# One fused attention and feed-forward kernel, its planner's cost of tiling changes on TensorE and of weight-load issues, and an order made anew

## The chip, the cores and the metric

The kernel runs on one core of one Trainium2 chip. The metric is the device time of one execution in microseconds (us). The kernel before took 1262.62 us, the median of three runs (1257.67 to 1267.32).

## The reference

Masked attention over 8 batches, 8 heads, 576 positions and 64 features, and behind it a feed-forward layer with a rational activation (512 to 2048 to 512):

```python
scores = scale * np.matmul(q, k.transpose(0, 1, 3, 2))
thresh = np.max(scores, axis=-1, keepdims=True) - tau
scores = np.where(scores >= thresh, scores, -1000000000.0)
...
attn = attn / (np.sum(attn, axis=-1, keepdims=True) + 1e-09)
return np.matmul(attn, v).astype(np.float32)
...
h = x @ w_in
P = a[0] + a[1] * h + a[2] * h2 + a[3] * h3
Q = 1.0 + np.abs(b[0]) * np.abs(h) + np.abs(b[1]) * h2
g = P / (Q + 1e-06)
return (g @ w_out).astype(np.float32)
```

Here x is the attention output with the heads laid side by side, 4608 rows of 512. All inputs and the output are float32.

## The kernel before, in words

**Work.** Heads are taken in pairs; `bp` counts the 32 pairs (8 batches of 4). The 576 positions are four tiles of 128 and a remainder of 64. One *unit* is one pair and one tile of 128 query positions (`unit_ops`). Its score matmuls (`f_qk`, line 810) contract over 64 features, so each of the two heads uses 64 rows of TensorE: the profile shows the form 64*128. The remainder units (line 800) hold both heads in one weight tile and run as 128*128. VectorE takes the row maxima (L818), ScalarE subtracts and masks (L833) and takes the exponential with its sum (L837). The scaled probabilities are split into a high and a low half-precision part: `hi` on ScalarE (L347) or VectorE (L349), the low part on VectorE (L859). Both are transposed by DMAs on SyncE's queue (`f_tp`, L869). For the first pairs (`is_plain`) the transposition runs on TensorE instead (`f_tr`, L882 and L887) and is copied out of PSUM (`f_ev`). The weighted sum over V (`f_av`, L928; `f_avp`, L912) fills 64 columns for each head: the form 128*64. It is made for two full tiles together.

The feed-forward layer takes 256 rows at a time (`moe_ops`): the first matmul (`f_g1`, L1045) uses w_in as high and low halves, a chain of VectorE and ScalarE operations (L1054 to L1095) makes the rational function, and the second matmul (`f_g2`, L1104) uses w_out in two float32 parts. The weights arrive as 64-bit words: `decode_ops` loads a tile of them by a DMA on GpSimd's queue (`load`, L546 and L582) and turns it into float32 on ScalarE and VectorE, in buffers of the pool `t` that the feed-forward chain uses later. `scale_ops` finds power-of-two scales by a maximum, a diagonal matrix (L442) and one small matmul (`f_all`, L446).

**Order.** No operation is emitted when it is written down. `op(engine, duration, key, function, ...)` records it, with the operations it needs, the buffers it takes and those it gives back. `Plan.order` then simulates the engines: at each step it takes, for each engine, the operation that can start first (with ties inside `TOL` decided by the smaller key), and emits them in that order. The order on each engine and on each DMA queue is therefore fixed in advance, and the chip executes each queue in order. An operation's key is its position in the series of units plus a number from the table `TURN` (one for each call of `begin`: one for each weight tile, V load, Q and K load, unit and feed-forward step) and one from `KIND` (one for each sort of operation), both in thousandths of a unit.

**Choice of engine.** An operation listed in `FLEX` can go to ScalarE or VectorE. `sooner` compares, for both, the start plus the duration times that engine's price: `EARLY` before the planned time `EARLY_END`, `PRICE` behind it.

**Durations.** Before the change a score unit is booked with 1.36 us (remainder: 1.12), a weighted sum with 1.86 us (remainder 0.69; in the plain form 2.36 and 0.76), whatever stands beside it. A weight load is booked with 2.5 us on the issuing queue `GD`, 1.9 us (times 1.25) on the wire and 2.0 us (plus 0.3) to its landing. `f_warm` (L1248) fills planned idle time of TensorE with small matmuls up to the planned time 400.

Of the kernel before, what the change touches and what calls it, by code (L numbers as in the profile page):

```python
# [77 lines left out]
        "ev": {"ACT": 0.465, "DVE": 0.6}, "ev1": {"ACT": 0.156, "DVE": 0.196}, "A": {"ACT": 0.565, "DVE": 0.341},  # L78
        "gh": {"ACT": 0.51, "DVE": 0.33}, "wh": {"ACT": 0.57, "DVE": 0.38}}

EARLY = {"ACT": 1.6309, "DVE": 3.9296}
EARLY_END = 714.5248
PRICE = {"ACT": 0.9171, "DVE": 2.3360}

TURN = [
# [22 lines left out]
KIND = [  # L108
# [4 lines left out]

TOL = {"PE": 0, "ACT": 0.129, "DVE": 0.1, "POOL": 0.1, "DMA": 0, "GD": 0}
WARM, WARM_ONE, WARM_LONG, WARM_END = 0.6, 0.22, 3.0, 400.0

BEGIN = 1.4
WIRE, LATER = 1.25, 0.3


# [20 lines left out]
class Plan:  # L141
# [17 lines left out]
    def pool(self, name, n):  # L159
        self.pools[name] = [(0.0, i) for i in range(n)]  # L160

    def op(self, eng, dur, key, fn, after=(), take=(), drop=(), wire=None):
        engs = {eng: dur} if isinstance(eng, str) else eng
        o = Op(engs, key, fn, [x for x in after if x is not None], list(take), list(drop))
        o.wire = wire and (wire[0] * WIRE, wire[1] + LATER)
        o.turn, o.kind = self.turn, self.kinds.setdefault(fn.__code__, len(self.kinds))
        turn = TURN[o.turn] / 1000 if o.turn < len(TURN) else 0.0
        o.key += turn
        o.key += KIND[o.kind] / 1000 if o.kind < len(KIND) else 0.0
        o.rank = self.rank + turn  # L170
        self.ops.append(o)
        return o
# [20 lines left out]
    def order(self):  # L193
# [16 lines left out]
                if h.pool in line:  # L210
                    line[h.pool].append(h)
        done, busy = [], dict.fromkeys(engines, 0.0)
        left, wire = len(self.ops), 0.0
        while left:
            best = None
            for e in engines:
# [11 lines left out]
                if not starts:  # L228
                    continue
                first = min(t for t, _ in starts)  # L230
                starts = sorted([x for x in starts if x[0] <= first + TOL[e]] if all(len(o.engs) == 1 for _, o in starts)
                                else starts, key=lambda x: (x[1].key, x[1].n))
# [4 lines left out]
                first = min(t for t, _ in keep)  # L237
                t, o = min(((t, o) for t, o in keep if t <= first + TOL[e]), key=lambda x: (x[1].key, x[1].n))
# [2 lines left out]
            assert best is not None, "no op can start"  # L241
            t, o, e = best
            o.eng, o.dur = e, o.engs[e]
            for x in o.engs:
                can[x].remove(o)
            if e == "PE" and self.warm is not None and t < WARM_END:
# [10 lines left out]
            if o.wire is not None:  # L257
                wire = max(wire, t + BEGIN) + o.wire[0]
# [39 lines left out]
def masked_attention_rational_ffn(  # L298
# [27 lines left out]
    op = plan.op  # L326
# [156 lines left out]
    def decode_ops(i, key, load, hold, dst=None):  # L483


        box = {}
        plan.begin(key - AHEAD_RANK)
        ht = Hold("u", 1)

        def ld():  # L490
            if not loaded:

                for x in KKs[0][:, 0:1], QQs[0][:, 0:1]:
                    nc.gpsimd.tensor_scalar(cf[:, 15:16], x, 1.0, 1.0, ALU.mult, ALU.mult)
            if len(loaded) >= AHEAD and plan.now - loaded[-AHEAD][1] < RECENT:


                nc.gpsimd.tensor_scalar(cf[0:1, 15:16], loaded[-AHEAD][0][0:1, 0, 1:2].bitcast(F32), 1.0, 1.0, ALU.mult, ALU.mult)
            box["rw"] = load()
            loaded.append((box["rw"], plan.now))  # L500

        def f1():


            box["w"] = place(ht)
            nc.scalar.activation(box["w"], box["rw"][:, :, 1].bitcast(F32), AF.Prelu, scale=REBIAS, alpha=-2.0 ** 32)

        def f2():
            nc.scalar.activation(box["rw"][:, :, 0], box["rw"][:, :, 0].bitcast(U32), AF.Copy, scale=2.0 ** -29)

        def f4():
            t = box["w"].bitcast(I32)
            nc.vector.tensor_single_scalar(t, t, 3, ALU.logical_shift_left)

        def f6():
            t = box["w"].bitcast(I32)
            if dst is None:
                tensor_tensor(box["rw"][:, :, 1], t, box["rw"][:, :, 0], ALU.add)
                box["w"] = box["rw"][:, :, 1].bitcast(F32)
            else:  # L520
                tensor_tensor(dst.bitcast(I32), t, box["rw"][:, :, 0], ALU.add)

        l = op("GD", 2.5, key - 2.0, ld, (), [hold], wire=(1.9, 2.0))
        if i < NC:
            first_loads.append(l)
        o1 = op("ACT", 0.567, key, f1, [l], [ht])
        o2 = op("ACT", 0.568, key, f2, [l])
        o4 = op("DVE", 0.335, key, f4, [o1])
        o6 = op(FLEX["f6"], 0, key, f6, [o4, o2], (), [ht] if dst is None else [ht, hold])
        return o6, box  # L530
# [7 lines left out]
    for i in range(NW):  # L538
        pieces = []
        for c in range(NC):  # L540
            n = i * NC + c
            hold = Hold("t", 1)
# [5 lines left out]
            key = w_key(i, c)  # L548
# [8 lines left out]
        key = w_key(i, NC)  # L557
# [19 lines left out]
    for f in range(NF):  # L577
        hold = Hold("t", 1)
# [5 lines left out]
        key = w_key(f // NC, NC + f % NC)  # L584
# [88 lines left out]
    def v_low(bp):  # L673
        if bp not in v_done:
            p, o, vl, vc, vhi = v_ops[bp]
            o = op(FLEX["vl"], 0, p + 0.1, vl, [o] + plain_av.get(bp, []))
            v_done[bp] = op("DVE", 0.25, p + 0.15, vc, [o], (), [vhi])
        return v_done[bp]
# [88 lines left out]
    def unit_ops(bp, t):  # L767
# [180 lines left out]
        sh = dict.fromkeys(heads, Hold("s", nh, B2 if single else B3))  # L948
        ex, mk = {}, {}
        need = k_done[bp] + q_done[bp]  # L950
        qk = op("PE", 1.36 if full else 1.12, p, f_qk, need, [sh[0]], [kh, qh] * nh)
        if full:
            mx = op("DVE", 1.255, p + 0.1, lambda: f_max(None), [qk], [st_hold])
        else:
# [40 lines left out]
            xh_hold[ck] = Hold("x" if ck[0] == "m" else "xr", 8 * NFP)  # L995
            first = [xh_hold[ck]]
        if plain:
            av = op("PE", 2.36 if full else 0.76, p + 1.2, f_avp, two["tp"] + [v_loaded[bp], x_first.get(ck)], [bh] + first, [two["pT"], vh_[bp]])
            plain_av.setdefault(bp, []).append(av)
        else:  # L1000
            av = op("PE", 1.86 if full else 0.69, p + 1.2, f_av, two["tp"] + [v_low(bp), x_first.get(ck)], [bh] + first, [two["pT"], vh_[bp]])
        x_first.setdefault(ck, av)
        xh = op(FLEX["xh" if full else "xhr"], 0, p + 1.4, f_xh, [av, isx_done["up"]] + ([x_done[ck][0]] if not first else []), (), [bh])
        xl = op("DVE", 0.335 if full else 0.134, p + 1.5, f_xl, [xh], (), [bh])
# [286 lines left out]
```

## Time and profile before

| | |
|---|---|
| median of three runs | 1262.62 us (1257.67 to 1267.32) |
| the profiled execution | 1266.8 us, span 1265.0 us |
| mean granted TensorE clock in it | 0.991 |
| matmul instructions on TensorE | 9650, as many weight loads |
| packets moved by DMA | 338603, 138.54 MB |

The span goes from the first to the last instruction of the profiled execution; its own time holds a little more, and it is one execution, not the median. Lines are those of the kernel file; the helpers `times` (L347 on ScalarE, L349 on VectorE) and `copy` (L339, L341) record one line for all who call them. A float32 matmul stands in the trace as two records, one in half precision as one. Matmuls overlap, so the time that a run of them takes is read from its start to the start of what follows.

### The profile page before, as it was taken

Reading aid. Unit: us, or ns where it says so; the run is one execution under the profiler, and the core shown is the slowest. Engines: PE = TensorE matmul, PEld = TensorE weight load, DVE = VectorE, ACT = ScalarE, POOL = GpSimd, SP = SyncE. Lnnn points to the kernel's source line nnn. Section 1 sums busy time; section 2 is a strip of 40 time slices with the busy share of each in tenths; the row PEclk is TensorE's granted clock in tenths of the full one; section 3 lists DMA queues with packets and bytes.
Section 4 is the critical chain, followed back from the end, with each engine's and each line's share of the span. In section 5 each row is a group of like instructions: output and inputs, shape, how many; then the busy total and the mean of one; then the engine's idle time right before and its main releaser. Section 6 shows DMA issues by size and latency. Waiting matters only on the chain. (4 is left out here: it accounts for less than half of the span.)

```text
span 1265.0 us, 25738 instructions
## 1 busy us (share of the span) xinstructions
PE 1226.9 (97%) x9650; PEld 961.6 (76%) x9650; DVE 1188.0 (94%) x1830; ACT 1118.3 (88%) x2185; POOL 97.8 (8%) x217
## 2 busy tenths in 40 slices
PE   8899999999999999999999999999999989999998
PEld 6677777777777777767777777777777767778886
DVE  6999899999999999999999899999999979998787
ACT  7999999999989899988898999899999979895564
POOL 4110000010001100101001100021001100000000
PEclk9999999999999999999999999999999989999999
DMA  6454644675556654665664666667456664542000
GB/s 193 136 167 129 149 81 85 134 151 119 114 95 146 126 110 102 124 121 89 124 116 80 131 125 96 122 120 139 90 112 125 132 109 88 116 88 45 18 17 17
DMA packets 338603, 138.54 MB, mean 110 GB/s; under 512 B 312624, under 2 KB 321712, under 8 KB 338480
## 3 DMA queue, kind: packets, MB, share of 16 engines
q1 hardware_dynamic: 326656, 103.40, 43.9%
q0 software_dynamic: 11072, 32.91, 8.9%
q8 instruction: 76, 1.25, 0.4%
q10 hardware_dynamic: 752, 0.59, 0.2%
q14 instruction: 47, 0.39, 0.1%
HBM read 52.17 MB, written 9.44 MB: 49 GB/s over the span
## 5 line engine op out<-in xcount | busy, mean ns | idle before, releaser
L1104 PE MATMUL banks<-wp,g 128*128 128x512 f32 x1728 | 449.1, 408 | 3.2 <-DVE g L1095 1.7
L1104 PEld LDWEIGHTS banks<-wp,g 128*128 128x128 f32 x1728 | 317.1, 191 | 82.6 <-DVE g L1095 4.4
L1045 PEld LDWEIGHTS <-wi 128*128 128x128 f16 x3456 | 328.8, 98 | 65.3 <-issue 23.3
L1045 PE MATMUL banks<-x,wi 128*128 128x256 f16 x3072 | 360.4, 274 | 3.8 <-ACT t L1054 3.3
L837 ACT ACTIVATE e<-e,cf 128x576 f32<-128x576 f32 x288 | 222.3, 779 | 0.2
L859 DVE SCALAR_TENSOR_TENSOR e<-e,st,hi 128x576 f16<-128x576 f32 x252 | 204.3, 811 | 7.2 <-ACT hi L347 6.5
L833 ACT ACTIVATE e<-banks,st 128x576 f32<-128x576 f32 x288 | 207.2, 739 | 4.2 <-DMA pT<-e 1.9
L347 ACT ACTIVATE hi<-e,st 128x576 f16<-128x576 f32 x225 | 171.0, 770 | 30.2 <-DVE st L848 25.3
L810 PE MATMUL banks<-KK,QQ 64*128 64x64 f32 (+1 forms) x1024 | 175.5, 455 | 7.4 <-ACT e L833 4.5
L818 DVE TENSOR_REDUCE st<-banks 128x2 f32<-128x1152 f32 x128 | 172.3, 1346 | 8.0 <-PE banks L810 7.2
L810 PEld LDWEIGHTS banks<-KK,QQ 64*128 64x128 f32 x1024 | 115.1, 188 | 77.0 <-issue 46.9
L1054 ACT ACTIVATE t<-banks,hsc 128x512 f32<-128x512 f32 (+1 forms) x192 | 106.6, 577 | 26.0 <-PE banks L1045 16.4
L928 PE MATMUL banks<-pT,V 128*64 128x256 f16 (+1 forms) x2520 | 121.7, 250 | 2.6 <-DVE xr L944 2.4
L928 PEld LDWEIGHTS <-V 128*64 128x64 f16 x2520 | 103.7, 111 | 23.3 <-issue 18.8
L1081 DVE SCALAR_TENSOR_TENSOR t<-t,co,t 128x1024 f32<-128x1024 f32 (+1 forms) x73 | 92.2, 1263 | 18.7 <-ACT t L1075 18.6
L1072 ACT ACTIVATE t<-t,co 128x1024 f32<-128x1024 f32 (+1 forms) x73 | 82.9, 1136 | 28.3 <-DVE t L1078 27.0
L1095 DVE TENSOR_TENSOR g<-t,g 128x512 fp32r<-128x512 f32 x144 | 95.2, 683 | 0.8 <-ACT g L339 0.7
L1087 DVE SCALAR_TENSOR_TENSOR t<-t,co,t 128x1024 f32<-128x1024 f32 (+1 forms) x73 | 92.2, 1264 | 0.6
L1065 DVE SCALAR_TENSOR_TENSOR t<-t,co 128x1024 f32<-128x1024 f32 (+1 forms) x73 | 92.2, 1263 | 0.3 <-ACT t L1054 0.3
L1068 DVE SCALAR_TENSOR_TENSOR t<-t,co 128x1024 f32<-128x1024 f32 (+1 forms) x73 | 92.2, 1263 | 0.0
L1078 DVE SCALAR_TENSOR_TENSOR t<-t,co,t 128x1024 f32<-128x1024 f32 (+1 forms) x73 | 92.2, 1263 | 0.0
L1084 DVE SCALAR_TENSOR_TENSOR t<-t,t 128x1024 f32<-128x1024 f32 (+1 forms) x73 | 87.9, 1204 | 0.5
(116 smaller groups left out, 1183.5 us busy)
## 6 DMA issues: line engine op xcount, KB each, us to landing
KK<-in_kT_dram SPq DMA_DIRECT2D x108, 144.0 KB, 3.0
t<-in_w_in_dram POOLq DMA_DIRECT2D x16, 512.0 KB, 4.9
t<-in_w_out_dram POOLq DMA_DIRECT2D x16, 512.0 KB, 4.8
V<-in_v_dram POOLq DMA_DIRECT2D x28, 256.0 KB, 4.4
out_dram<-u POOLq DMA_DIRECT2D x26, 256.0 KB, 3.0
QQ<-in_qT_dram SPq DMA_DIRECT2D x72, 64.0 KB, 2.3
pT<-hi SPq DMA_TRANSPOSE x140, 3.3
pT<-e SPq DMA_TRANSPOSE x140, 3.3
```

What stands on the lines that cost most here:

```text
L347: nc.scalar.activation(dst, src, AF.Identity, scale=factor)
L810: mm = nc.tensor.matmul(s[:, d0:d0 + n], QQ[r, t * P:(t + 1) * P], KK[r, k0:k0 + n], **one)
L818: nc.vector.tensor_reduce(box["st"][:, 0:2], box["both"], AX.X, ALU.max, negate=True)
L833: nc.scalar.activation(ev(hh), box["s"][hh], AF.Prelu, scale=SCALE, bias=box["st"][:, 2 + hh:3 + hh], alpha=STEEP)
L837: nc.scalar.activation(e, e, AF.Exp, scale=passes, accum_out=box["st"][:, 4 + hh:5 + hh])
L859: nc.vector.scalar_tensor_tensor(box["lo"][:, c], ev(hh), box["st"][:, 6 + hh:7 + hh], box["hi"][:, c], ALU.mult, ALU.subtract)
L928: nc.tensor.matmul(dst, V[:, c * P + hh * D:c * P + (hh + 1) * D], rhs, start=c == 0 and n == 0, stop=c == NT and n == 2)
L1045: nc.tensor.matmul(d, wi_tile(c, f0 + j, hl), x[:, c, :], start=c == 0 and n == 0, stop=c == NC - 1 and n == 2)
L1054: nc.scalar.activation(box["h3"][:, 2 * k:2 * k + 2, sl], psv[:, :, sl], AF.Identity, scale=hsc[:, b2, g:g + 1])
L1065: nc.vector.scalar_tensor_tensor(box["r"], box["h"], a2, box["h"], ALU.add, ALU.mult)
L1095: nc.vector.tensor_tensor(fr(g[:, 1]), box["r"][:, k * GW:(k + 1) * GW], g[:, 0], ALU.subtract)
L1104: nc.tensor.matmul(acc[tt], fr(g[:, x]), fr(wo[f][y]), start=begins and j == n == 0, stop=ends and j == nb - 1 and n == 2)
```

## The change

The planner gets a cost for a change of TensorE's tiling. Each operation has a `mode`: 1 for score units, 2 for weighted sums, 0 for all others. When TensorE's next operation has another mode than the last, `TURNS` = 0.093 us is added to its duration. The booked durations of score units and weighted sums are each lowered by 0.185 us (about twice 0.093). A weight load is booked with 0.65 us on the issuing queue instead of 2.5, and with 0.3 us more to the landing. The tables `TURN` (367 numbers) and `KIND` (65) and the four prices are replaced, so that the order on all engines is a new one. No emitted operation is edited.

```diff
-EARLY = {"ACT": 1.6309, "DVE": 3.9296}
+EARLY = {"ACT": 1.7163, "DVE": 3.8382}
 EARLY_END = 714.5248
-PRICE = {"ACT": 0.9171, "DVE": 2.3360}
+PRICE = {"ACT": 1.0826, "DVE": 2.3926}
...
+TURNS = 0.093
...
-    def op(self, eng, dur, key, fn, after=(), take=(), drop=(), wire=None):
+    def op(self, eng, dur, key, fn, after=(), take=(), drop=(), wire=None, mode=0):
...
+        o.mode = mode
...
-        left, wire = len(self.ops), 0.0
+        left, wire, mode = len(self.ops), 0.0, 0
...
             o.eng, o.dur = e, o.engs[e]
+            if e == "PE":
+                o.dur += TURNS if o.mode != mode else 0.0
+                mode = o.mode
...
-        l = op("GD", 2.5, key - 2.0, ld, (), [hold], wire=(1.9, 2.0))
+        l = op("GD", 0.65, key - 2.0, ld, (), [hold], wire=(1.9, 2.3))
...
-        qk = op("PE", 1.36 if full else 1.12, p, f_qk, need, [sh[0]], [kh, qh] * nh)
+        qk = op("PE", 1.175 if full else 0.935, p, f_qk, need, [sh[0]], [kh, qh] * nh, mode=1)
...
-            av = op("PE", 2.36 if full else 0.76, p + 1.2, f_avp, two["tp"] + [v_loaded[bp], x_first.get(ck)], [bh] + first, [two["pT"], vh_[bp]])
+            av = op("PE", 2.175 if full else 0.575, p + 1.2, f_avp, two["tp"] + [v_loaded[bp], x_first.get(ck)], [bh] + first, [two["pT"], vh_[bp]], mode=2)
...
-            av = op("PE", 1.86 if full else 0.69, p + 1.2, f_av, two["tp"] + [v_low(bp), x_first.get(ck)], [bh] + first, [two["pT"], vh_[bp]])
+            av = op("PE", 1.675 if full else 0.505, p + 1.2, f_av, two["tp"] + [v_low(bp), x_first.get(ck)], [bh] + first, [two["pT"], vh_[bp]], mode=2)
```

Of the tables, the entries of the same kinds before and after show how far keys move (thousandths of a unit): score units -1392 and -1418, weighted sums -1204 and -4381, the first feed-forward matmul 152 and -1087, the second 727 and 215.

52 rows, old and new, of tables (KIND, TURN) are left out of this document.

## The prediction

> **What bounds the kernel now.** I read the page's busy times first, then busy time by stage, then the clock inside short stretches, TensorE's waits, and its instructions in order of time.
>
> ```profile
> span 1265.0 us, 25738 instructions
> PE 1226.9 (97%) x9650; PEld 961.6 (76%) x9650; DVE 1188.0 (94%) x1830; ACT 1118.3 (88%) x2185; POOL 97.8 (8%) x217
> ```
>
> The stage table (start:end, length, then busy time of TensorE, its weight loads, VectorE, ScalarE and GpSimd, with the number of instructions in brackets, the granted TensorE clock, the DMA share and GB/s) shows where the missing 3% lies:
>
> ```profile
> 0.00:217.00 217.00, 200.81 (x1531) 157.34 (x1531) 195.18 (x416) 203.34 (x432) 29.06 (x65) 0.99 0.52 137
> 217.00:1014.00 797.00, 784.64 (x6377) 612.52 (x6377) 776.32 (x1134) 737.89 (x1441) 66.53 (x148) 0.99 0.61 117
> 1014.00:1030.00 16.00, 11.74 (x61) 8.62 (x61) 11.29 (x24) 9.11 (x19) 0.00 (x0) 0.79 0.90 147
> 1030.00:1260.00 230.00, 229.23 (x1684) 183.10 (x1682) 205.17 (x259) 167.28 (x297) 2.21 (x4) 1.00 0.28 55
> ```
>
> TensorE is busy for 229.23 of the 230 us from 1030 to 1260, where its work ends, so every microsecond taken off its queue there or earlier comes off the end. It idles 217.00 - 200.81 = 16.2 us in the first stage, 797.00 - 784.64 = 12.4 us in the second and 4.3 us in the third. VectorE follows closely: in the second stage it is only 784.64 - 776.32 = 8.3 us less busy than TensorE. So TensorE is the bound, with VectorE right behind it.
>
> The waits behind those gaps (engine, line, whom it waited for, us in total, times, longest):
>
> ```profile
> PE banks L446 <- DVE u L442: 4.9, 2, 4.3
> PE banks L810 <- ACT e L833: 4.5, 9, 1.7
> PE banks L882 <- ACT pT L339: 3.4, 5, 1.1
> PE banks L1045 <- ACT t L1054: 3.3, 3, 1.8
> PE banks L810 <- DMA KK<-in_kT_dram: 2.6, 2, 2.1
> PE banks L928 <- DVE xr L944: 2.4, 1, 2.4
> ```
>
> They are a few long ones, each of another kind, not a steady drip. Each is followed by a stretch of low clock (eighth column here: the granted clock, after the five busy times):
>
> ```profile
> 559.00:564.00 5.00, 5.00 (x39) 3.35 (x35) 4.95 (x9) 2.72 (x5) 0.00 (x0) 0.66 0.35 69
> 692.00:697.00 5.00, 5.00 (x35) 3.97 (x28) 4.46 (x7) 3.57 (x10) 2.12 (x5) 0.66 0.94 181
> 744.00:748.00 4.00, 3.48 (x9) 2.84 (x10) 4.00 (x8) 3.55 (x7) 2.16 (x4) 0.57 0.86 203
> 1020.00:1028.00 8.00, 6.67 (x27) 4.89 (x28) 7.12 (x19) 6.78 (x14) 0.00 (x0) 0.57 0.75 164
> ```
>
> Lost clock is length x (1 - clock): 1.7 + 1.7 + 1.7 + 3.4 = 8.5 us. With the idle 12.4 + 4.3 = 16.7 us, the middle of the kernel (217 to 1030) loses 25.2 us to stalls, in four clusters of about 6 us.
>
> **The change, part by part.** No instruction is added or taken away by the edit itself, except that the number of filler matmuls (L1248) follows the planner's gaps. What changes is the order on every engine, and which of two engines takes an optional operation.
>
> First, the tiling changes. TensorE in order of time (start, us, line, count of records; the first and last tiled runs enclose a gapless stretch):
>
> ```profile
> 4.66 5.30 PE L810 MATMUL banks<-KK,QQ 64*128 64x64 f32 x16
> ...
> 311.82 1.35 PE L810 MATMUL banks<-KK,QQ 64*128 64x64 f32 x8
> 313.10 1.48 PE L1045 MATMUL banks<-x,wi 128*128 128x256 f16 x12
> 314.34 3.05 PE L1104 MATMUL banks<-wp,g 128*128 128x512 f32 x12
> 317.31 1.83 PE L928 MATMUL banks<-pT,V 128*64 128x256 f16 x30
> 319.07 1.35 PE L810 MATMUL banks<-KK,QQ 64*128 64x64 f32 x8
> 320.35 3.07 PE L1104 MATMUL banks<-wp,g 128*128 128x512 f32 x12
> 323.26 3.45 PE L1045 MATMUL banks<-x,wi 128*128 128x256 f16 x30
> 326.64 1.83 PE L928 MATMUL banks<-pT,V 128*64 128x256 f16 x30
> 328.40 1.35 PE L810 MATMUL banks<-KK,QQ 64*128 64x64 f32 x8
> 329.68 4.10 PE L1045 MATMUL banks<-x,wi 128*128 128x256 f16 x36
> 333.54 1.17 PE L1104 MATMUL banks<-wp,g 128*128 128x512 f32 x3
> ...
> 1154.79 1.83 PE L928 MATMUL banks<-pT,V 128*64 128x256 f16 x30
> 1156.55 3.06 PE L1104 MATMUL banks<-wp,g 128*128 128x512 f32 x12
> ```
>
> I take the time of a run as its start to the next run's start. A score unit (L810) takes 1.27 to 1.28 us and a weighted sum (L928, full) 1.76 us, whether a tiled or an untiled run stands ahead or behind. So leaving a tiling costs nothing beyond what those two figures hold. Entering does: L1045 takes 3.86 us for 36 and 1.24 us for 12 ahead of L1104, 0.109 us each, so 30 would take 3.20; ahead of the weighted sum 30 take 3.38, 0.17 us more. L1104 x12 takes 2.91 us ahead of L1045 and 2.97 ahead of the weighted sum, 0.06 more. A tiled run placed directly behind another therefore saves 0.06 to 0.17 us. Where the untiled neighbours stand about evenly I take 0.13 for one saved entry, from the upper part of that span, because the second L1104 figure follows an L1045 run and the first does not.
>
> [...]
>
> How many entries? Over the whole timeline, from the row at 4.66 to that at 1154.79, I count 224 runs of score units and weighted sums, 176 of them entered from an untiled run and 48 directly behind another tiled one. If every run had one tiled neighbour, 112 entries would be left: 64 x 0.13 = 8.3 us is the most, and none is the least. The pick among ready operations on TensorE does not look at the tiling; the new cost is added after the pick. Pairs arise only because the keys are new. So I take about half, 35 entries, and 35 x 0.13 = 4.5 us off.
>
> The accounting is not quite the chip's. The remainder scores are counted as tiled like the others, though the trace has them as 128*128:
>
> ```profile
> L800 PE MATMUL banks<-KK,QQ 128*128 128x512 f32 x64 | 33.4, 604 | 0.3 <-ACT st L842 0.3
> L1248 PE MATMUL banks<-ident 128*128 128x128 f32 x162 | 26.4, 309 | 1.4 <-POOL ident masks.py:199 1.4
> ```
>
> With two records of this form a unit these are 32 units: if each is placed as a free neighbour and is not one, at most 32 x 0.13 = 4.2 us of the credit is false. I take this as contained in "half".
>
> Second, the weight loads. The planner now books 0.65 us instead of 2.5 us on the issuing queue for each of 32 loads, and 0.3 us more to the landing. The trace has
>
> ```profile
> 63.73 0.53 POOL L582 DMA_DIRECT2D t<-in_w_out_dram  x1 [13.67 <-ACT t L509]
> ...
> POOL t L546 <- ACT t L509: 18.1, 1, 18.1
> ```
>
> An issue takes 0.53 us, so the new figure is the better one; but the queue waits for buffers that ScalarE and VectorE have to give back, up to 18.1 us at once, and no row of TensorE's waits names a weight load. Earlier issue is covered by that wait. I cost it at nothing. If the cover went and an earlier weight load delayed a load of V, K or Q, the nearest row is the 2.1 us that scores waited for K: bounds -2 and +2 us. In the same first stage the filler matmuls take 26.4 us and the idle time is 16.2 us; a new order can shift some of this either way, and I take nothing, bounds -5 and +5.
>
> Third, the order itself. V loads, Q and K loads, scale computations and whole units move on every queue, so the four clusters of stalls will not come at the same places. For the long one (4.3 us at L446) the scale matmul stood in TensorE's queue ahead of operations that were ready, with the whole queue behind it waiting for VectorE's L442; for the next K load it was SP's queue in which the transposes stood ahead. A moved operation meets the same in-order queues, so new waits arise too. Bounds: none left, -25.2 us; as many again, +25.2 us. I take half a cluster, -3 us, nearer to no change, because nothing in the cost model that touches those four waits is altered.
>
> Fourth, the prices. Where an operation may go to either engine, its time is weighed by EARLY (first part) or PRICE. VectorE's price over ScalarE's goes from 2.41 to 2.24 and from 2.55 to 2.21: a little more work for VectorE, below its slack of 8.3 us. I take nothing; the far end is the third rival.
>
> Sum: 1266.8 us for the profiled execution (span 1265.0 and 1.8 around it) - 4.5 - 3 = 1259.3. That execution lies 4.2 us above the median of the runs, 1262.62, so against the median the forecast is 1255.1 us.
>
> **The rivals.** (1) It does not do what it says: the pick ignores the tiling, TensorE's runs are paired as before, and stalls return in other places at the same total: 1262.6 us. For it speaks that a unit's scores become ready only when ScalarE (L833) has freed its banks, so that pairs are set by readiness; against it, that 48 pairs stand already.
>
> (2) The stalls go: three of the four middle clusters don't return, 0.75 x 25.2 = 18.9 us, with the 4.5 us of entries: 1262.6 - 23.4 = 1239.2 us. For it: the stretch from 1030 to 1260 runs nearly without a gap. Against it: each cluster has its own cause. [...]
>
> (3) Slower: VectorE becomes the bound between 217 and 1014. The place is the choice of engine for the scaled probabilities:
>
> ```profile
> L349 DVE TENSOR_SCALAR hi<-e,st 128x576 f16<-128x576 f32 x27 | 14.2, 524 | 0.3
> ...
> L347 ACT ACTIVATE hi<-e,st 128x576 f16<-128x576 f32 x225 | 171.0, 770 | 30.2 <-DVE st L848 25.3
> ```
>
> Each one that moves puts 0.524 us on VectorE. From 8.3 / 0.524 = 16 moved on, VectorE sets the pace. If 60 of the 225 move, that is 31.4 - 8.3 = 23.1 us, less the 4.5: 1281.2 us. For it: the price ratio moves that way in both parts. Against it: the advantage that ScalarE must keep (0.427 and 0.667 us in the planner, times the prices) falls only from 0.59 to 0.49 and from 0.39 to 0.30, which should move few.
>
> **How the numbers follow.** A measurement of this kernel can tell about 1% from no change: its three runs lie 9.7 us apart, so under 1250 is faster and over 1275 slower. The forecast gets 0.47, (1) 0.14, (2) 0.24, (3) 0.15. About a fifth of the forecast's share lies under 1250 and a little over 1275, so faster is 0.24 + 0.10 = 0.34, slower 0.15 + 0.01 = 0.16, same 0.50. The forecast's own range is 1246 to 1268; the range reaches toward the rivals, from 1237 to 1277, and leaves out the far ends of (2) and (3).
>
> **What would show it.** Right: entries from an untiled run fall from 176 to about 141, with L810 and L928 runs unchanged at 1.28 and 1.76 us; TensorE's busy time falls by some 4 us; two to four clusters of stalls with low clock in the middle, at new places; hi on VectorE below about 40. Wrong: as many entries as before; middle idle and lost clock together under 10 us or over 40; VectorE busy longer than TensorE in the middle; a weight load among TensorE's waits, or a first stage longer by more than 5 us.

## The result, and the profile after

The changed kernel takes 1274.39 us, the median of nine runs (1271.12 to 1279.67). The kernel before, run beside it, takes 1267.32 us (nine runs with those shown above, 1257.67 to 1276.86). The ratio is 1.006, with a 95% interval of 1.0034 to 1.0086: some 7 us slower, clear of noise though under 1%, where the forecast was 7.5 us faster. The profiled execution took 1271.1 us, the fastest of the nine, so it shows only 4.3 us of the difference in its span.

In the changed kernel's profile L810 is L815, L928 is L933, L1045 is L1050, L1104 is L1109, L833 is L838, L711 is L716 and L869 is L874; the experiments shift a few lines more. The head of its page:

```profile
span 1269.3 us, 25726 instructions
PE 1225.9 (97%) x9646; PEld 961.8 (76%) x9646; DVE 1195.5 (94%) x1839; ACT 1108.3 (87%) x2175; POOL 98.4 (8%) x217
```

TensorE's busy time is 1225.9 us against 1226.9. Some of a busy time is low clock (at a clock of 0.50 the score unit's row at 708.40 us of the changed kernel lasts 2.50 us, elsewhere 1.35). The mean clock of the kernel before and the changed one (two lines of the view of cores):

```profile
core 0: 1265.0 us, clock 0.991
```

```profile
core 0: 1269.3 us, clock 0.990
```

Take span x (1 - clock) off each: 1226.9 - 11.4 = 1215.5 and 1225.9 - 12.7 = 1213.2 us. The new order leaves TensorE's work as it was, within 2.3 us. Counted over the whole timeline as in the prediction, entries into a tiling went from 176 to 179, and tiled runs directly behind another from 48 to 45. A score unit and a weighted sum still take 1.27 and 1.76 us (changed kernel, TensorE in order of time):

```profile
327.98 1.35 PE L815 MATMUL banks<-KK,QQ 64*128 64x64 f32 x8
329.25 1.83 PE L933 MATMUL banks<-pT,V 128*64 128x256 f16 x30
331.01 2.14 PE L1050 MATMUL banks<-x,wi 128*128 128x256 f16 x18
```

So the 4.3 us are waits (span less busy time goes from 38.1 to 43.4 us). The stages, with the columns of the prediction's table:

```profile
0.00:217.00 217.00, 198.86 (x1511) 156.01 (x1512) 192.17 (x416) 200.75 (x425) 29.47 (x65) 0.98 0.49 134
217.00:1014.00 797.00, 778.98 (x6292) 606.09 (x6290) 775.41 (x1124) 722.28 (x1419) 64.37 (x143) 0.99 0.60 116
1014.00:1030.00 16.00, 16.00 (x124) 12.34 (x123) 15.96 (x26) 14.91 (x31) 2.35 (x5) 1.00 0.95 151
1030.00:1264.00 234.00, 231.35 (x1724) 187.04 (x1723) 211.93 (x276) 169.63 (x301) 2.22 (x4) 1.00 0.30 59
```

TensorE idles 2.0 us more in the first stage, 5.7 us more from 217 to 1014, 1.9 us more in the last stage, and no longer around 1017, where the kernel before had idled 4.3 us and lost 3.4 us of clock. What it waits for (the longest groups):

```profile
PE banks L815 <- ACT e L838: 11.4, 13, 4.4
PE banks L933 <- DVE V L753: 3.1, 1, 3.1
PE banks L451 <- DVE u L447: 3.0, 3, 1.8
```

Scores waiting for ScalarE to free their banks (L838) went from 4.5 to 11.4 us, and one wait of 4.4 us leads. It sits at 704 us. First TensorE, then ScalarE at that place:

```profile
698.56 5.42 PE L1050 MATMUL banks<-x,wi 128*128 128x256 f16 x48
708.40 2.50 PE L815 MATMUL banks<-KK,QQ 64*128 64x64 f32 x8 [4.43 <-ACT e L838]
```

```profile
701.44 0.69 ACT L1059 ACTIVATE t<-banks,hsc 128x512 f32<-128x512 f32 x1
706.89 0.74 ACT L716 ACTIVATE u<-V 128x640 bf16<-128x640 f32 x1 [4.76 <-DMA V<-in_v_dram]
707.54 0.19 ACT L716 ACTIVATION_READ_ACCUMULATOR u<-V 128x1 f32 x1
707.63 0.72 ACT L838 ACTIVATE e<-banks,st 128x576 f32<-128x576 f32 x1
```

ScalarE's queue stands 4.76 us at the absolute maximum of a V tile whose load has not landed, and L838, which would free the scores' banks, stands behind it. After the 4.43 us comes a stretch of half clock (0.50 from 708.40 to 710.90 us). What was in flight, on GpSimd's queue and on SyncE's:

```profile
692.82 0.76 POOL L701 DMA_DIRECT2D V<-in_v_dram  x1 [0.24 <-issue]
693.57 1.05 POOL L705 DMA_DIRECT2D V<-in_v_dram  x2
694.66 0.33 POOL L695 MEMSET V<- 64x64 f32 x2
694.94 0.80 POOL L701 DMA_DIRECT2D V<-in_v_dram  x1
695.73 1.04 POOL L705 DMA_DIRECT2D V<-in_v_dram  x2
```

```profile
692.22 1.30 SPq L874 DMA_TRANSPOSE pT<-hi  x1
693.57 1.25 SPq L661 DMA_DIRECT2D KK<-in_kT_dram  x2
694.92 1.30 SPq L874 DMA_TRANSPOSE pT<-e  x1
701.48 4.89 SPq L874 DMA_TRANSPOSE pT<-hi  x2
706.46 2.89 SPq L874 DMA_TRANSPOSE pT<-e  x2
```

Two V loads, a K load and two transposes start within 4 us. The view of line L701 gives the landing of V loads as shortest, median and longest; the longest is the one at 694.94. The transpose at 694.92 took 11.6 us to land; the transpose, the V load and the K load that started up to 2.7 us earlier took 5.7 to 6.4 us. From 702 to 706 us the DMA share is 1.00 and 62 GB/s are moved (last two columns):

```profile
DMA to landing us min/median/max: 2.8/3.9/11.1
```

```profile
702.00:706.00 4.00, 1.97 (x19) 1.52 (x16) 2.70 (x3) 0.13 (x1) 0.00 (x0) 1.00 1.00 62
```

### The profile page after: what moved, and what is told of

Same layout as the page of the kernel before. It is cut to its first block, busy times and chain, and to the rows that moved or that the text cites. A ratio compares the mean times of both kernels' runs of the same rounds, so it can differ in the third digit from the quotient of the medians.

```text
span 1269.3 us, 25726 instructions
## 1 busy us (share of the span) xinstructions
PE 1225.9 (97%) x9646; PEld 961.8 (76%) x9646; DVE 1195.5 (94%) x1839; ACT 1108.3 (87%) x2175; POOL 98.4 (8%) x217
## 5 line engine op out<-in xcount | busy, mean ns | idle before, releaser
L1109 PE MATMUL banks<-wp,g 128*128 128x512 f32 x1728 | 443.5, 405 | 6.5 <-DVE g L1100 2.9
L1109 PEld LDWEIGHTS banks<-wp,g 128*128 128x128 f32 x1728 | 316.0, 189 | 86.4 <-DVE g L1100 5.7
L1050 PEld LDWEIGHTS <-wi 128*128 128x128 f16 x3456 | 328.6, 98 | 62.1 <-issue 20.3
L1050 PE MATMUL banks<-x,wi 128*128 128x256 f16 x3072 | 359.1, 273 | 2.6 <-ACT t L1059 2.5
L838 ACT ACTIVATE e<-banks,st 128x576 f32<-128x576 f32 x288 | 206.3, 740 | 10.9 <-DMA pT<-e 6.8
L352 ACT ACTIVATE hi<-e,st 128x576 f16<-128x576 f32 x214 | 162.9, 770 | 33.3 <-DVE st L853 28.0
L815 PE MATMUL banks<-KK,QQ 64*128 64x512 f32 (+1 forms) x1024 | 174.9, 453 | 15.4 <-ACT e L838 11.4
L815 PEld LDWEIGHTS banks<-KK,QQ 64*128 64x128 f32 x1024 | 114.8, 187 | 85.5 <-issue 47.0
L933 PE MATMUL banks<-pT,V 128*64 128x256 f16 (+1 forms) x2520 | 123.9, 252 | 4.2 <-DVE V L753 3.1
L933 PEld LDWEIGHTS <-V 128*64 128x64 f16 x2520 | 105.3, 112 | 24.3 <-issue 16.0
```

What stands on the lines that cost most here:

```text
L352: nc.scalar.activation(dst, src, AF.Identity, scale=factor)
L815: mm = nc.tensor.matmul(s[:, d0:d0 + n], QQ[r, t * P:(t + 1) * P], KK[r, k0:k0 + n], **one)
L838: nc.scalar.activation(ev(hh), box["s"][hh], AF.Prelu, scale=SCALE, bias=box["st"][:, 2 + hh:3 + hh], alpha=STEEP)
L933: nc.tensor.matmul(dst, V[:, c * P + hh * D:c * P + (hh + 1) * D], rhs, start=c == 0 and n == 0, stop=c == NT and n == 2)
L1050: nc.tensor.matmul(d, wi_tile(c, f0 + j, hl), x[:, c, :], start=c == 0 and n == 0, stop=c == NC - 1 and n == 2)
L1109: nc.tensor.matmul(acc[tt], fr(g[:, x]), fr(wo[f][y]), start=begins and j == n == 0, stop=ends and j == nb - 1 and n == 2)
```

## The experiments

Three theories stood against each other. Theory A: the pairing of tiled runs did not change, because the pick does not look at the tiling, and single stalls in in-order queues decide. Theory B: the new prices, with their shift to VectorE, are the cause (in the first pair of runs: the new tables and prices as a whole, with an accounting that helps). Theory C: the price of a change of tiling was misread, and leaving a tiling costs time too. All ratios are to the kernel before on the same chip, with 95% intervals.

**The accounting alone, and the tables alone.** The first takes the new durations, `TURNS` and modes with the old `TURN`, `KIND` and prices; the second the new tables and prices with the old durations:

```diff
# accounting alone, against the kernel before (tables and prices untouched)
+TURNS = 0.093
...
-        l = op("GD", 2.5, key - 2.0, ld, (), [hold], wire=(1.9, 2.0))
+        l = op("GD", 0.65, key - 2.0, ld, (), [hold], wire=(1.9, 2.3))
...
-        qk = op("PE", 1.36 if full else 1.12, p, f_qk, need, [sh[0]], [kh, qh] * nh)
+        qk = op("PE", 1.175 if full else 0.935, p, f_qk, need, [sh[0]], [kh, qh] * nh, mode=1)
...
# tables alone, against the changed kernel
-TURNS = 0.093
+TURNS = 0.0
...
+        l = op("GD", 2.5, key - 2.0, ld, (), [hold], wire=(1.9, 2.0))
...
+        qk = op("PE", 1.36 if full else 1.12, p, f_qk, need, [sh[0]], [kh, qh] * nh, mode=1)
...
```

> The tables and prices of the kernel before, with all of the new accounting (tiling changes and weight loads). Theory A (the pick doesn't look at the tiling, the tables belong to one set of durations, and stalls decide the time): 170 to 185 entries into a tiling as before, but many more waits on TensorE, idle over 50 us, time 1285 to 1320 us. Theory B (the accounting itself is what improves the order, and the new prices and tables spoil it): 1250 to 1262 us. If the accounting does nothing at all: 1267 us.

> The new tables and prices, with the old durations and no cost for a change of tiling. Theory A: again tables with durations that they do not belong to, idle over 50 us, 1285 to 1320 us. Theory B (tables and prices alone are the loss, through VectorE's added 7.5 us): about 1274 us as the changed kernel, VectorE's busy time about 1195 us in both theories.

Measured: 1331.78 us, ratio 1.0517 (1.0471 to 1.0564), and 1317.48 us, ratio 1.0405 (1.0353 to 1.0458). The page of the first:

```profile
span 1326.3 us, 25788 instructions
PE 1245.0 (94%) x9680; PEld 969.4 (73%) x9680; DVE 1195.5 (90%) x1822; ACT 1119.8 (84%) x2193; POOL 98.8 (7%) x218
```

TensorE is 81 us short of the span, where it was 38 in the kernel before; entries are 173 and 174 in the two runs. The loss is even larger than expected for the first. A table belongs to the durations that it was made with: half the change costs 50 to 65 us, and the other half gives it back, no more. This also means that the two halves cannot be valued one by one.

**The price of an entry.** In the order of the kernel before, the untiled operation that comes next is put between two tiled ones:

```diff
+    def parted(seq, reach):
...
+            if o.tag in ("qk", "av") and pe and seq[pe[0]].tag in ("qk", "av"):
+                to = next((j for j in pe[1:] if not seq[j].tag), None)
...
+                    x = seq.pop(to)
+                    seq.insert(pe[0], x)
...
+    seq = parted(plan.order(), 8.0)
```

> The order of the kernel before, with an untiled operation moved between two tiled ones that stand side by side, wherever its inputs allow: 38 more entries into a tiling (176 to 214), nothing else changed. Theory A (an entry costs 0.06 to 0.17 us, leaving nothing): 2.3 to 6.5 us more, best guess 5 us, ratio 1.004, all of it in TensorE's busy time. [...] If the weight loads hide it: under 1 us.

Measured: 1272.01 us, ratio 1.0044 (1.0017 to 1.0071), 5.6 us for 38 entries, 0.15 us each (0.06 to 0.24 by the interval). Its page, mean clock and one place (L813 is the score unit, L931 the weighted sum):

```profile
span 1267.2 us, 25732 instructions
PE 1230.4 (97%) x9650; PEld 956.6 (75%) x9650; DVE 1189.1 (94%) x1830; ACT 1118.9 (88%) x2185; POOL 98.1 (8%) x217
```

```profile
core 0: 1267.2 us, clock 0.993
```

```profile
451.16 1.35 PE L813 MATMUL banks<-KK,QQ 64*128 64x64 f32 x8
452.44 0.83 PE L1050 MATMUL banks<-x,wi 128*128 128x256 f16 x6
453.20 1.83 PE L931 MATMUL banks<-pT,V 128*64 128x256 f16 x30
```

Busy time less lost clock is 1230.4 - 8.9 = 1221.5 us against 1215.5: 6.0 us more, 0.16 per entry. In the rows L1050 x6 takes 0.76 us ahead of the weighted sum, not 0.58 or so as ahead of L1109, and L813 stays at 1.28. The price of the entry accounts for all that was measured, and no cost of leaving shows: theory C is out, the price stood.

**All maxima of V later.** In the order of the kernel before, each V maximum comes 4 us later, and what needs it as far as it must:

```diff
+            at[o] = max([o.start + (by if o.tag == tag else 0.0)] +
+                        [at[x] + x.dur for x in back[o] if at[x] > x.start])
+        return sorted(seq, key=lambda o: at[o])
+
+    seq = pushed(plan.order(), "vmax", 4.0)
```

> The order of the kernel before, with the absolute maximum of V moved 4 us later in its engine's queue (and what needs it as far as it must), so that ScalarE does not stand and wait for a V load that lands late. Theory A (the 4.3 us gap at 1017 us with its half clock comes from ScalarE's queue standing at that operation): 4.3 + 3.4 = 7.7 us less where it recurs, best guess 6 us, ratio 0.995, waits of ScalarE for V near 0. Theory B: no change, ratio 0.998 to 1.002. If the moved chain of scales is missed later: slower by the wait that takes its place.

Measured: 1279.8 us, ratio 1.0112 (1.0074 to 1.015). The last sentence of the expectation came true: ScalarE no longer waited for V at that place of the order, but the scale chain behind the maxima was missed elsewhere (ScalarE's wait for sx is 7.9 us in five waits, at L349; in the kernel before 0.7 in three, at L347). In the profiled execution the V load in question (at 1029 us in this run) landed after 3.6 us, so ScalarE would not have stood there in any case. The edit was too broad, and as a test of theory A it is void.

**VectorE's share.** The mirror pair moves 11 scaled probabilities and 15 casts of g to the other engine, at their place in the order:

```diff
+    seq = moved(plan.order(), [("hi", 11), ("gh", 15)], "DVE", "ACT")
```

> The changed kernel's order, with 11 of its 38 scaled probabilities and 15 of its 48 casts of g on VectorE given to ScalarE at their place in the order: the shares of the kernel before (27 and 33). Theory B (the price shift makes VectorE the bound, 7.5 us more of it cost the 7 us): 4 to 7 us less, 1259 to 1262 where the kernel before has 1266. Theory A (shares lie within the slack; single stalls and the entries decide): within 3 us of the changed kernel, ratio to the kernel before 1.003 to 1.009.

> The mirror: the order of the kernel before, with 11 scaled probabilities and 15 casts of g moved from ScalarE to VectorE, the shares of the changed kernel (38 and 48). Theory B: 4 to 7 us more, ratio 1.003 to 1.006. Theory A: within 3 us, ratio 0.998 to 1.002. An operation at a fixed place can also be late on its new engine, which would make both mirrors slower.

Measured: 1280.12 us, ratio 1.0102 (1.0062 to 1.0143), for the changed kernel with the old shares; 1273.05 us, ratio 1.0049 (1.0016 to 1.0082), for the kernel before with the new ones. The second is slower than what it was made from; the first lies 0.004 above the changed kernel's ratio, which the two intervals do not settle. Giving VectorE's work back does not give the time back. But each moved operation is also at a place that was not made for its engine, so the second run fits theory B as well as the late place; alone the pair does not settle B.

**Second profiles.**

> The kernel before once more, for a second profile. Theory A: the long stall at 1017 us (ScalarE's queue standing for a V load) comes or not by how late that load lands, while the shorter ones (555, 689, 740 us) recur; time 1258 to 1275.

> The changed kernel once more, for a second profile. Theory A: the 4.4 us stall at 704 us (a V load landing after 11 us) need not recur; idle time before 217 us of about 17 us and waits of scores for ScalarE (L838) recur; time 1271 to 1280.

The kernel before, again (1258.71 us), at the place of its long stall:

```profile
1014.00:1030.00 16.00, 16.00 (x120) 12.44 (x117) 15.86 (x33) 14.80 (x30) 0.00 (x0) 1.00 0.61 117
```

No idle time and full clock, where in the first profile ScalarE had stood for a V load:

```profile
1019.28 0.74 ACT L711 ACTIVATE u<-V 128x640 bf16<-128x640 f32 x1 [4.92 <-DMA V<-in_v_dram]
```

That stall comes and goes. The changed kernel, again (1273.38 us), at its own:

```profile
707.50 2.50 PE L815 MATMUL banks<-KK,QQ 64*128 64x64 f32 x8 [4.42 <-ACT e L838]
```

It recurs to 10 ns, against what I had expected ("need not recur"). So does the wait for V at L753 (3.10 us at 894 us, here 2.89). Idle time of the first stage does not tell the kernels apart: it is 18.3 us in this second profile of the kernel before and 17.1 in that of the changed one. The recurring long stall is the difference between the two orders that the next runs had to test.

**One maximum moved.** In the changed kernel only the maximum at which ScalarE stood comes 8 us later; one operation of the whole order changes place.

```diff
+            mine = by if o.tag == "vmax" and first < o.start < last else 0.0
...
+    seq = pushed(plan.order(), 692.0, 693.0, 8.0)
```

> The changed kernel with a single operation moved: the absolute maximum of the V tile whose load landed 11 us after its issue in both profiles (the one for which ScalarE stood still at 702 us) comes 8 us later in ScalarE's queue; its result is wanted 36 us later. Theory A (the new order's loss is this recurring stall): 4.4 us of idle time and 3.4 us of half clock go, 7.8 us less than the changed kernel, 1265 to 1267 us, ratio to the kernel before 0.998 to 1.002. Rival: the queue stands for the transposes or K loads of the same moment and the wait only takes another name: ratio stays at 1.004 to 1.009.

Measured: 1274.47 us, ratio 1.0058 (1.0028 to 1.0088): nothing gained. ScalarE and TensorE there (L841 is the old L838, L818 the score unit):

```profile
704.83 0.67 ACT L1064 ACTIVATE t<-banks,hsc 128x512 f32<-128x512 f32 x1
709.90 0.74 ACT L841 ACTIVATE e<-banks,st 128x576 f32<-128x576 f32 x1 [4.41 <-DMA pT<-e]
```

```profile
710.69 1.34 PE L818 MATMUL banks<-KK,QQ 64*128 64x64 f32 x8 [3.79 <-ACT e L841]
```

The rival of that expectation holds: the wait took another name. With V's maximum out of the way, L841 waits for a transpose that is just as late (12.0 us to its landing, the V load beside it 11.4), since it gives back the buffer of e. So the late thing is not the V load alone but also the transpose that started with it.

**The last two maxima of the kernel before, 4 us later.** The same edit at 990 to 1020 in the kernel before.

> The kernel before with the maxima of the last two V tiles (one of them is where ScalarE stood 4.9 us at 1014 us in its first profile, and not in its second) 4 us later, and the scale chain behind them as far as it must. Theory A: 7.7 us less in those executions in which that load lands late, nothing in the others: the slowest runs go, median 1 to 4 us less, ratio 0.996 to 1.000. Rival (as in the run that moved all maxima): the scale chain is missed and the time grows, ratio over 1.002.

Measured: 1267.12 us (1262.48 to 1270.86), ratio 1.0017 (0.999 to 1.0043). No gain. The slowest runs did not show up (none of 12 over 1271 us, where the kernel before reached 1275.89 in 23 runs beside it), and neither did the fastest. In the profiled execution the V load landed after 3.6 us, so it does not show what the edit does to a late one; it does show the scale chain late, at L349 on ScalarE:

```profile
1021.76 1.55 ACT L349 ACTIVATE u<-V,sx 128x640 f16<-128x640 f32 x2 [2.24 <-DVE sx L457]
```

**The loads apart.** In the changed kernel the second of the two V loads waits for the score unit planned next, and its maximum comes after that:

```diff
+        def later():
+            tc.add_manual_dep(nc.gpsimd.nop().ins, last_scores[0].ins.name, ORDERED, reason="apart")
+            issue()
+        load.fn = later
```

> The changed kernel with the second of the two V loads that start 2.1 us apart (692.8 and 694.9 us in its profile) held back on GpSimd's queue until the score unit at 704 us has run, and its maximum moved behind that in ScalarE's queue; nothing else. Theory A, as the run with one operation moved left it (not ScalarE's wait for V, but the DMA transfers of that moment are late: loads and transposes that start together land after 11 us): the transposes land in 4 to 6 us again, the 4.4 us stall and its 3.4 us of half clock go, 1266 to 1268 us, ratio 1.000 to 1.003. Rival (the transposes are late for another reason, or the burst is only put off): a stall of 3 us or more stays between 700 and 720 us, ratio 1.004 to 1.009.

Measured: 1269.09 us, ratio 1.0014 (0.9984 to 1.0043). The 30 us from just before the burst on, in the changed kernel and in this one, where the same work comes some 10 us later:

```profile
690.00:720.00 30.00, 25.57 (x205) 19.56 (x204) 22.65 (x32) 20.55 (x45) 4.17 (x10) 0.89 0.63 89
```

```profile
700.00:730.00 30.00, 30.00 (x250) 23.30 (x249) 29.43 (x40) 25.97 (x55) 4.59 (x10) 1.00 0.65 127
```

and SyncE's queue in this one:

```profile
702.02 1.30 SPq L880 DMA_TRANSPOSE pT<-hi  x1
703.37 1.29 SPq L664 DMA_DIRECT2D KK<-in_kT_dram  x2
704.75 2.15 SPq L880 DMA_TRANSPOSE pT<-e  x1
710.72 2.81 SPq L880 DMA_TRANSPOSE pT<-hi  x2
713.62 2.81 SPq L880 DMA_TRANSPOSE pT<-e  x2
```

The same transposes and the K load start at the same distances, one V load is gone from among them, and at this place the stall and its low clock are gone: 4.4 us idle and 30 x 0.11 = 3.3 us of clock less. The transpose at 704.75 landed after 5.4 us where it took 11.6, and the next pair is issued in 2.81 us where it took 4.89. From 1.006 to 1.0014 is 0.0046 of the time, 5.8 us; with the two intervals that is 5.8 give or take 5, so shown, but not sharply. What is left, 0.0014 or 1.8 us, may be nothing and may be some 5 us.

The profiled execution of this run does not show the gain in its total: it took 1273.92 us, the second slowest of its twelve. From 217 to 1030 us it idles 17.8 us and loses 6.8 us of clock, 24.6 us together, and the changed kernel's profile has 18.0 + 6.8 = 24.8 us. Another wait of the same kind stands at 592 us, ahead of the place of the edit, ScalarE's queue again at a maximum of V (first TensorE, then ScalarE):

```profile
592.00 2.50 PE L820 MATMUL banks<-KK,QQ 64*128 64x64 f32 x8 [3.68 <-ACT e L844]
```

```profile
588.33 0.74 ACT L719 ACTIVATE u<-V 128x640 bf16<-128x640 f32 x1 [3.67 <-DMA V<-in_v_dram]
```

In the first profile of the changed kernel TensorE waits 0.81 us there, in the second less than that, in the run with one maximum moved 3.36 us. So the new order has a stall that comes and goes too, and one profile cannot price the burst; the twelve times can, within the 5 us above. The wait for V at L753 near 894 us stands in all four of these profiles of the new order (2.89 to 3.28 us; in the first the clock from 896 to 902 us, behind it, is 0.75); no run took it out.

No version that was run beats the kernel before.

## Why the prediction was wrong

**The bound** was right: TensorE's work sets the time, and what changed is how long it waits.

**The price of an entry** was right: 0.13 us forecast, 0.15 to 0.16 measured. That leaving costs nothing further was right too (1.28 us for the score unit at 451.16 us with an untiled run put behind it, as before).

**The number of entries** is the first step that failed. I took "about half, 35 entries", 4.5 us; it is 3 more entries, so the term is 0.4 us of loss. No fewer entries than before was one of the signs of being wrong that I had named. I had written the reason for it myself, that the pick does not look at the tiling, and then still took the middle of the bounds. The bounds came from geometry (every run next to another), not from anything that moves two runs together. The row that should have weighed more is the wait of scores for ScalarE: a unit becomes ready when its banks are freed. That readiness alone prevents pairs was argued and not tried.

**The false credit** of the remainder scores was contained in "half", and did not matter, since there was no credit.

**The weight loads** at nothing held: first-stage idle time rose by 2.0 us from profile to profile, no more than the 2.1 us by which the two profiles of the kernel before differ, and no weight load is among TensorE's longest waits.

**The stalls** are the second step that failed, and the larger one. I took "half a cluster, -3 us". One cluster of the four, at 1017 us, came in one profile of the kernel before and not in the other, which I could not know from one profile, and the new order has one that recurs: a burst of V loads, K load and transposes at 693 us, 5.8 us by the run that takes a load out of it. Idle time and lost clock from 217 to 1030 us were 25.2 us in the first profile of the kernel before and 12.4 + 3.4 = 15.8 in the second; in the changed kernel they are 18.0 + 6.8 = 24.8 and 20.2 + 8.4 = 28.6. On the average of two profiles each the term is some 6 us of loss, not 3 us of gain. The bound (as many stalls again, 25.2 us) held; the sign was taken from nothing. In the prediction I named for the longest stall a matmul ahead of ready ones in TensorE's queue. The queue that stood, there at 1014 us (4.92 us) and in the changed kernel at 702 us (4.76 us), was ScalarE's, at a V load that had not landed. That each wait is followed by low clock was read too broadly as well: behind the 1.77 us at 579 us the clock stays at 1.00 (567 to 690 us).

**The prices** at nothing held within what was measured: hi on VectorE went from 27 to 38 (below the 40 named),

```profile
L354 DVE TENSOR_SCALAR hi<-e,st 128x576 f16<-128x576 f32 x38 | 19.5, 514 | 0.2
```

and VectorE's busy time by 7.5 us over the whole kernel. From 217 to 1014, where its slack was 8.3 us, its busy time is 0.9 us lower, and TensorE's 5.7 us, so the slack there is now 3.6 us. With the burst gone, 1.0014 is left for this and all else, so the third rival is not the main cause; that it costs up to 5 us (the interval's end) stays open.

**The rivals.** The first, same pairing and stalls at other places, describes what happened; its price, "at the same total", missed the 7 us. A wait that takes the place of another came up in three of the experiments that moved maxima of V.

## What to carry to other kernels

A cost put into a planner makes an event rarer only if the rule that picks can act on it (without that it still changes the order, as the run with the accounting alone shows, but not toward fewer entries: 173 against 176); look at the pick before crediting the cost, and count the events (here 176 and 179 entries) rather than the bounds. The times of these two orders, written out in advance, differ by a few places where an in-order queue stands for a transfer that lands later than the planner books (4.76 us at 702 us for a V load that landed after 11.1); more than one profile is needed to tell which of these recur, and two can still miss one that comes and goes, as at 592 us here. If moving the waiting operation away only renames the wait, look at what all the late transfers have in common.

## What the runs showed of the hardware

In the changed kernel the transpose at 694.92 us and the V load at 694.94 us landed after 11.6 and 11.1 us (median of the V loads 3.9), and from 702 to 706 us 62 GB/s were moved at a DMA share of 1.00. With that V load held back, the same transpose landed after 5.4 us, and the 30 us from the burst on moved 127 GB/s at a DMA share of 0.65, against 89 GB/s at 0.63.

What makes them late is open. Two V loads are not needed for it: at 1008 us of the kernel before (SyncE's queue, then GpSimd's) one V load, started next to a transpose, landed after 9.8 us in the first profile, and in the second, started as close to it, after 3.7 us:

```profile
1008.85 1.80 SPq L869 DMA_TRANSPOSE pT<-e  x1
```

```profile
1008.86 0.79 POOL L696 DMA_DIRECT2D V<-in_v_dram  x1 [0.22 <-issue]
```

The start at the same instant as a transpose is a rival to the number of transfers. I counted it in the traces of all 13 profiles, behind 217 us and by the first DMA of each V load: 13 of 312 started within 0.05 us of a transpose, and 9 of these landed after more than 7 us; of the other 299 it was 7. The profiles share their orders, so these are not 13 separate cases, and the run that held the load back parted it from the transpose as well. No run moved a load by a fraction of a microsecond, which would tell the two apart.
